# Up products of two half blocks at once in a fused retention and feed-forward kernel

## The chip, the cores and the metric

The kernel runs on one core of one Trainium2 chip. The core has a matrix engine (TensorE, PE in the profile; its weight loads are listed apart as PEld), three engines for elementwise work (VectorE or DVE, ScalarE or ACT, GpSimd or POOL) and SyncE (SP), which here only starts transfers. Each engine takes its instructions in the order of its own queue and waits on semaphores for the others. Matrix products are written to PSUM, 8 banks of 512 float32 in each of 128 partitions; everything else lies in SBUF. The metric is the time of one execution on the device in microseconds (us), taken as the median of the runs.

## The reference

Retention over 4 batches, 8 heads, 768 tokens and head dimension 64 gives a matrix of 3072 tokens by 512. A feed-forward layer follows, 512 to 2048 and back, with g = h - tanh(h) in between. The change lies in the feed-forward layer.

```python
def _attn_ref(q, k, v):
    ...
    for t in range(S):
        state = gamma[None, :, None, None] * state + np.einsum('bhd,bhe->bhde', k[:, :, t], v[:, :, t])
        y[:, :, t] = scale * np.einsum('bhd,bhde->bhe', q[:, :, t], state)

def _moe_ref(x, w_in, w_out):          # x: 3072 x 512, w_in: 512 x 2048, w_out: 2048 x 512
    h = x @ w_in
    g = h - np.tanh(h)
    return (g @ w_out).astype(np.float32)
```

## The kernel before

**Tiling.** The 3072 tokens are 6 blocks of 512, each of two half blocks n of 256 tokens (n = 0 to 11). The 2048 inner columns are 8 pairs m2 of two 128-column groups. A tile (n, m2) is h for 256 tokens and 256 inner columns: one PSUM bank, 128 partitions by 512. For each tile there is an up product (x times w_in), the elementwise part ("shrink", h - tanh(h)) that leaves g in SBUF, and a down product (g times w_out), which is added up in PSUM over the 8 tiles of a half block (a "run") to 256 tokens by 512 output columns. The inputs' retention part and the weights' preparation run early, beside half blocks 0 to 3; the half blocks 4 to 11 that concern us have nothing else beside them after the first steps.

**Seven products for eight.** From half block 4 on (FAST, FAST_UP), both products use a scheme that multiplies 2 x 2 blocks with seven block products and some sums (Winograd's form of Strassen's method). In the up product, numbers 1 to 7 name the products: up_weights (L750) makes sums of weight blocks once per m2, up_tokens (L761) sums of token blocks once per half block, both on POOL. fast_up (L773) issues products 1, 5, 7, 6 to the four quarters of the tile's bank, each as two calls for the two halves of the contraction, 128 columns wide. Then up_take (L782) copies the bank to SBUF on ACT, up_pairs (L785) adds two quarters of the copy pairwise on POOL, products 2, 3, 4 are added onto the bank, and up_add (L790) adds the POOL result on DVE. The down product has the same seven: fast_sums (L615) makes four sums of g's quarters on POOL, fast_products (L661) issues seven products of 256 columns into half-bank accumulators, and sums_of (L674) and fast_end (L705) combine the accumulators at the end of a run: a copy p1 on ACT, seven adds on DVE, two stores on SP's queue. Of the adds, c11 and v come at once, the other five lie in the list `ending` and end_some (L735) takes one of them in each later step. fast_banks (L632) rotates the accumulators of successive runs over six banks: t (two banks in one tile), y (two), o (two single ones).

**The order.** Everything is recorded by hand (manual_schedule): the order in the source is the order in each engine's queue. The main loop (L989) does a step for each tile: products 1, 5, 7, 6 of this tile; the copy; the last factors of the tile before on ACT and DVE; the pair sums on POOL; the first four down products of the tile that is `lag` = 3 steps back; products 2, 3, 4; up_add; tanh and square; the end of the tile before (multiply, copy_predicated, fast_sums); the remaining three down products; one pending add; then the first DVE operations of this tile. After the last tile the remaining three tiles' down products follow. The very last of them goes through finish (L718), which orders its seven products so that each add can follow early, and takes the quarter c22 by way of ACT and POOL.

**The shrink chain.** For a tile, ACT does tanh, square (u), q0, q1 and large, three of them from u; DVE does th = h - tanh (L502), h = (q0 + C0) h (L506), g = (q1 + A C1) h (L515, shrink_last_factor), g = g u (L522) and copy_predicated (L523). q0 and q1 have one buffer each, u, th and large two. Names in the profile are cut of their numbers: h is a tile's bank, fast_head the ACT copy and its pair sums, fast_t, y and fast_o the accumulators, s the sums of g, sum the output rows.

## Time and profile before

| | |
|---|---|
| median of 3 runs | 696.62 us (696.27 to 698.77) |
| the profiled execution | 695.71 us, of which the span is 693.9 us |
| PE busy in the span | 685.8 us (99%), 6540 instructions |
| DVE, ACT, POOL busy | 523.8 us (75%), 432.6 us (62%), 348.1 us (50%) |
| granted TensorE clock | 1.00 |
| up records of 128 columns (L778) | 28 in each step of half blocks 4 to 11 |
| down records of 256 columns (L669) | 14 in each step of half blocks 4 to 11 |
| POOL 128x256 (L788), 128x512 (L208), 128x128 (L620) | 731, 1325, 458 ns |
| ACT 128x512 copy, tanh, square from u | 586, 598, 725 ns |
| DVE 128x512 L502, L506, L515, L522, L523 (from 500 us on) | 680, 689, 688, 736, 751 ns |
| DVE L793 (128x256), L795 (128x128) | 433, 329 ns |

The span runs from the first to the last instruction of the profiled execution; the execution's own time is 1.8 us longer. A busy time counts the instructions of an engine, not its waits. Matmuls are pipelined: the listed duration of one is longer than the spacing of two that follow each other, so the spacing (a group's time divided by its records) is what a product costs in a full queue. The product issued by one call in the code appears as two records. The other engines overlap a little too: an instruction can start about 0.1 us before the listed end of the one before it.

### The profile page before, as it was taken

The page shows a single profiled execution, that of the slowest core. Times are in us where ns is not written, and L with a number is a line of the kernel's source. Part 1 is how long each engine was busy: PE and PEld are TensorE (multiplying, and loading weights), DVE is VectorE, ACT ScalarE, POOL GpSimd, SP SyncE. Part 2 cuts the span into 40 slices and gives each one's busy share as a digit, 9 for nine tenths or more (in the row PEclk, how much of TensorE's full clock was granted, in tenths as well). Part 3 has the DMA queues.
Part 4 walks back from the last instruction along what each step waited for, and adds up shares of the span by engine and source line. Part 5 has one row for each costly group of instructions (what it writes and reads, how often), then busy time and mean ns, then how long its engine had stood idle before and what let it go on. Part 6 is the DMA issues. An engine that isn't in the chain of part 4 may idle for free.

```text
span 693.9 us, 16487 instructions
## 1 busy us (share of the span) xinstructions
PE 685.8 (99%) x6540; PEld 572.4 (82%) x6540; DVE 523.8 (75%) x894; ACT 432.6 (62%) x818; POOL 348.1 (50%) x517
## 2 busy tenths in 40 slices
PE   8999999999999999999999999999999999999997
PEld 5776666667667767789999999999999999999996
DVE  4999999988988965587777676676676776766775
ACT  4787577766867665555665556655556655556553
POOL 1632454454454677878853354453544543544333
PEclk9999999999999999999999999999999999999999
DMA  8992268869888657400000000000000000000001
GB/s 231 242 281 50 79 172 222 214 166 237 222 189 231 147 153 197 123 33 1 1 1 16 17 1 31 1 1 31 1 1 31 1 5 27 2 16 17 1 16 46
DMA packets 119548, 59.95 MB, mean 86 GB/s; under 512 B 101680, under 2 KB 112560, under 8 KB 119472
## 3 DMA queue, kind: packets, MB, share of 16 engines
q1 hardware_dynamic: 116880, 50.21, 27.9%
q10 hardware_dynamic: 2592, 8.69, 3.4%
q8 instruction: 51, 0.84, 0.5%
q14 instruction: 25, 0.20, 0.1%
HBM read 35.83 MB, written 14.68 MB: 73 GB/s over the span
## 4 chain that ended last, share of the span: by engine, by line
PE 94%; DVE 2%; DMA 2%; issue 1%; ACT 0%; POOL 0%; SPq 0%; POOLq 0%; DVEq 0%; ACTq 0%
PE h L778 28%; PE h L464 16%; PE o L531 16%; PE fast_t L669 10%; PE y L669 8%; PE fast_o L669 8%; PE y L398 3%; PE s L343 2%; PE s L349 1%; DMA k<-in_k_dram 1%; PE kqTp L298 1%; DMA v<-in_v_dram 1%; DMA q<-in_q_dram 0%; DVE a L356 0%; DVE g L523 0%
## 5 line engine op out<-in xcount | busy, mean ns | idle before, releaser
L477 ACT ACTIVATE th<-h 128x512 f32<-128x512 f32 x64 | 38.2, 598 | 141.9 <-DVE h L795 141.9
L620 POOL TENSOR_TENSOR s<-g 128x128 f32<-128x128 f32 x64 | 29.3, 458 | 191.6 <-DVE g L523 185.8
L464 PE MATMUL h<-xT,w 128*128 128x256 f32 x512 | 117.8, 382 | 0.2 <-POOL w L217 0.2
L531 PE MATMUL o<-w,g 128*128 128x512 f32 x256 | 116.5, 596 | 0.0
L464 PEld LDWEIGHTS h<-xT,w 128*128 128x128 f32 x512 | 95.9, 190 | 21.7 <-issue 9.1
L531 PEld LDWEIGHTS o<-w,g 128*128 128x128 f32 x256 | 47.5, 190 | 46.2 <-issue 42.8
L778 PEld LDWEIGHTS h<-xT,w 128*128 128x128 f32 x512 | 76.8, 191 | 8.4 <-ACT fast_head L783 1.0
L523 DVE COPY_PREDICATED g<-large,th 128x512 f32<-128x512 int32 x88 | 76.1, 864 | 9.0
L793 DVE TENSOR_TENSOR h<-h,fast_head 128x256 f32<-128x256 f32 x64 | 27.7, 433 | 68.5 <-PE h L778 65.8
L778 PE MATMUL h<-xT,w 128*128 128x128 f32 x512 | 78.3, 275 | 0.2 <-ACT fast_head L783 0.2
L502 DVE TENSOR_TENSOR th<-h,th 128x512 f32<-128x512 f32 x88 | 60.0, 682 | 18.0 <-ACT th L475 16.6
L515 DVE SCALAR_TENSOR_TENSOR g<-q,h 128x512 f32<-128x512 f32 x64 | 44.0, 688 | 36.5 <-ACT q L491 35.2
L778 PE MATMUL h<-x,w 128*128 128x128 f32 x448 | 68.3, 275 | 0.0
L483 ACT ACTIVATE q<-u,tab 128x512 f32<-128x512 f32 x88 | 63.8, 725 | 1.7
L208 POOL TENSOR_TENSOR low<-low,power 128x512 f32<-128x512 f32 x26 | 34.5, 1325 | 59.2 <-DVE power L201 46.2
L491 ACT ACTIVATE q<-u,tab 128x512 f32<-128x512 f32 x88 | 63.6, 723 | 0.0
L506 DVE SCALAR_TENSOR_TENSOR h<-q,h 128x512 f32<-128x512 f32 x88 | 60.7, 690 | 2.6 <-ACT q L483 2.6
L492 ACT ACTIVATE large<-u,tab 128x512 f32<-128x512 f32 x88 | 62.6, 712 | 0.0
L778 PEld LDWEIGHTS h<-x,w 128*128 128x128 f32 x448 | 59.0, 192 | 0.0
L783 ACT COPY fast_head<-h 128x512 f32<-128x512 f32 x64 | 37.5, 586 | 20.0 <-PE h L778 19.9
L522 DVE TENSOR_TENSOR g<-g,u 128x512 f32<-128x512 f32 x64 | 48.6, 759 | 0.0
L788 POOL TENSOR_TENSOR fast_head<-fast_head 128x256 f32<-128x256 f32 x64 | 46.7, 730 | 1.2 <-ACT fast_head L783 1.2
(197 smaller groups left out, 1494.8 us busy)
## 6 DMA issues: line engine op xcount, KB each, us to landing
rows<-apart ACTq DMA_DIRECT2D x16, 512.0 KB, 4.3
k<-in_k_dram SPq DMA_DIRECT2D x24, 256.0 KB, 4.3
q<-in_q_dram SPq DMA_DIRECT2D x24, 256.0 KB, 4.7
v<-in_v_dram SPq DMA_DIRECT2D x24, 256.0 KB, 5.5
raw<-in_moe_w_out_dram SPq DMA_DIRECT2D x12, 512.0 KB, 4.2
out_dram<-sum SPq DMA_DIRECT2D x22, 256.0 KB, 2.0
raw<-in_moe_w_in_dram SPq DMA_DIRECT2D x14, 256.0 KB, 4.1
raw<-in_moe_w_in_dram SPq DMA_DIRECT2D x28, 128.0 KB, 4.1
```

Of the source, the lines that this page charges most:

```text
L464: nc.tensor.matmul(hp, w1[:, c, ts(2 * m2 + i, P)], xT[n // 2][:, c, ts(n % 2, TH)], start=(begins and c == 0), stop=(c == NC - 1), skip_g ...
L483: nc.scalar.activation(q0, shrinking[n, m2][0], AF.Square, bias=bias0)
L491: nc.scalar.activation(q1, u, AF.Square, bias=bias1, scale=math.sqrt(A))
L492: nc.scalar.activation(large, u, AF.Relu, bias=bias_m)
L502: nc.vector.tensor_tensor(th, hp, th, op=ALU.subtract)
L506: nc.vector.scalar_tensor_tensor(hp, in0=shrinking[n, m2][2], scalar=C0, in1=hp, op0=ALU.add, op1=ALU.mult)
L522: nc.vector.tensor_tensor(flat, src, u, op=ALU.mult)
L523: nc.vector.copy_predicated(flat, large.bitcast(I32), th)
L531: nc.tensor.matmul(o_p[n, j], gT[n, m2][:, i, ts(j, P)], w2[:, 2 * m2 + i], start=(first and i == 0), stop=(last and i == 1))
L669: nc.tensor.matmul(accs[n][k], left[k - 1], right, start=first and k in (1, 6, 7, 4), stop=last, skip_group_check=True)
L778: nc.tensor.matmul(hps[n, m2][:, ts(PLACE[k], P)], s_of[m2][k - 1][:, c], x_of[n][k - 1][:, c], start=(k == 1 and c == 0), stop=(c == 1), ...
L788: nc.gpsimd.tensor_tensor(odd_room[1], first[:, :2], first[:, 3:1:-1], op=ALU.add)
```

## The change

The half blocks 8 to 11 (PAIRED = 8) leave the main loop and get a loop of their own over 16 "block steps": block b (4 and 5), m2 from 0 to 7, in which both half blocks of a block are made at once. The 2 x 2 scheme now splits the 512 tokens of the block into two halves of 256, not the 256 tokens of a half block into two of 128. So a product has 256 columns, and the seven products (14 calls) of a block step fill two banks, one for each half block, with the two inner groups side by side in each. The sums of tokens have four operations per block on 128x512, no longer eight on 128x256, and lie in part in the place of the block's own tokens. The copy is two ACT operations, the pair sums are one POOL operation of 128x512, and the adds are three on DVE of 128x256.

Down products are no longer tied to a tile: next_products(k) issues the next k of the queue of waiting tiles. In half blocks 6 and 7 a step issues 4 + 2 of them (before: 4 + 3). In a block step four are issued after products 1, 7, 5, 6, and more after 2, 4, 3: up to 6 in the first eight block steps and up to 10 in the last eight. They stop at the end of a run. What is left follows after the last block step. feed makes the POOL sums for up to three waiting tiles as soon as their g is there. As g tiles wait longer, new_g takes more room for them: the tokens of finished blocks and a buffer of v, and tiles whose products are done.

The sums at the end of a run are all queued at once in the block loop (end_some(len(ending))). fast_banks gives each run accumulators by name: runs 7, 8, 9 and 10 all have t0, y1, t1 and y0, and the last run has the two o banks and two new ones. For the last run, finish takes the last three tiles accumulator by accumulator, and queues each add behind the products of its accumulator; all seven adds are on DVE, c22 and c21 are stored by ACT's queue and c11 and c12 by SP's.

```diff
...
         hp = hps.pop((n, m2))
         q1 = shrinking[n, m2][3]
-        g = gT[n, m2] = gp.tile([P, 2, TH], F32, tag="g", name=f"g_{n}_{m2}")
+        g = gT[n, m2] = new_g(n, m2)
         dst = hp if n < FAST_UP else g.rearrange("p i t -> p (i t)")
         nc.vector.scalar_tensor_tensor(dst, in0=q1, scalar=A * C1, in1=hp, op0=ALU.add,
                                        op1=ALU.mult)
         shrinking[n, m2].append(dst)
+    units = []
+    def more_units():
+        def of(t):
+            for i in range(4):
+                yield t[:, i].rearrange("p (i t) -> p i t", i=2)
+        yield from of(xp.tile([P, NP, BLK * P], F32, tag="xT", name="g_x2"))
+        for i in range(4):
+            yield gp.tile([P, 2, TH], F32, tag="g", name=f"g_{i}")
+        v_ = inp.tile([P, BANK], F32, tag="v", name="g_v", bufs=4)
+        yield v_.rearrange("p (i t) -> p i t", i=2)
+        for i in range(3, NB - 1):
+            yield from of(xp.tile([P, NP, BLK * P], F32, tag="xT", name=f"g_x{i}"))
+    rooms_for_g = more_units()
+    def new_g(n, m2):
+        if n < PAIRED - 1:
+            return gp.tile([P, 2, TH], F32, tag="g", name=f"g_{n}_{m2}")
+        return units.pop(0) if units else next(rooms_for_g)
     def shrink_end(n, m2):
         u, th, _, _, large, src = shrinking.pop((n, m2))
...
     FAST = 4
+    PAIRED = 8
     PAIRS = NM // 2
     t_of = {}
...
-    spare = []
     accs = {}
+    fast_o = []
     def fast_banks(n):
-        if not spare:
+        if not fast_o:
             t = banks("t", "fast_t")
-            whole = y_banks.rearrange("p two r n t -> p r (two n t)")
-            o = [bank("o", "fast_o") for _ in range(2)]
-            spare.append([t[:, 0], t[:, 1], o[0], whole[:, 0], whole[:, 1]])
-            spare.append(o[1])
-        five, sixth = spare
+            y = y_banks.rearrange("p two r n t -> p r (two n t)")
+            fast_o.extend([bank("o", "fast_o") for _ in range(2)])
+            fast_o.append(dict(t0=t[:, 0], t1=t[:, 1], y0=y[:, 0], y1=y[:, 1],
+                               o0=fast_o[0], o1=fast_o[1]))
+        named = fast_o[2]
         if n == 2 * NB - 1:
-            five[1:3] = five[2], five[1]
-        first, second, third = five[:3]
-        spare[0] = five[3:] + [first, second, third]
+            named.update(h0=bank("h", "last_h"), h1=bank("h", "last_h"))
+        names = {
+            4: "t0 t1 o0 o1", 5: "y0 y1 t0 o1", 6: "t1 o1 o0 y0", 2 * NB - 1: "o0 o1 h0 h1",
+        }.get(n, "t0 y1 t1 y0")
+        first, second, third, sixth = (named[x] for x in names.split())
         acc = {1: first, 2: first, 5: second, 7: second, 3: third, 4: third, 6: sixth}
         right = {2: 1, 7: 1, 4: 1, 6: n % 2}
+        if n == 2 * NB - 1:
+            acc[3], right[3] = sixth, 0
         accs[n] = {k: b[:, ts(right.get(k, 0), TH)] for k, b in acc.items()}
-    def fast_order(n, first):
-        if not first:
-            return (1, 2, 4, 6, 7, 5, 3)
-        return (1, 2, 4, 3, 7, 6, 5) if n == 2 * NB - 1 else (1, 2, 7, 5, 4, 6, 3)
+    def fast_order(first):
+        return (1, 2, 7, 5, 4, 6, 3) if first else (1, 2, 4, 6, 7, 5, 3)
     def fast_down(n, m2, first, last, half=None):
-        some = fast_order(n, first)[{None: slice(7), 0: slice(4), 1: slice(4, 7)}[half]]
+        some = fast_order(first)[{None: slice(7), 0: slice(4), 1: slice(4, 7)}[half]]
         if first and 1 in some:
             fast_banks(n)
         fast_products(n, m2, first, last, some)
...
             "c21": lambda: add(c21, 4, w_, True), "c12": lambda: add(c12, 3, x_),
         }
...
                     store(int(x == "c21"))
             ending.append(step)
-    def finish(n, m2, first, last):
-        todo, store, late_c22 = None, None, None
+    def finish(n, some):
+        todo, store = sums_of(n)
         left, right = (ts(c, TH) for c in range(2))
-        for some, then in (((1, 2), ("p1", "c11")), ((6,), ("v",)), ((7, 5), ("w", "x")),
-                           ((4, 3), ("c21", "c12"))):
-            fast_products(n, m2, first, last, some)
-            if todo is None:
-                todo, store, late_c22 = sums_of(n)
+        for ks, then in (((1, 2), ("p1", "c11")), ((6,), ("v",)), ((7,), ("w",)),
+                         ((4,), ("c21",)), ((5,), ("x", "c22")), ((3,), ("c12",))):
+            for m2 in some:
+                fast_products(n, m2, False, m2 == PAIRS - 1, ks)
             for x in then:
                 todo[x]()
                 if x[0] == "c":
-                    store(int(x[1]) - 1, left if x[2] == "1" else right)
-                if x == "x":
-                    late_c22()
-        store(1, right, nc.scalar)
+                    store(int(x[1]) - 1, left if x[2] == "1" else right,
+                          nc.scalar if x in ("c22", "c21") else nc.sync)
     def end_some(n):
         for _ in range(min(n, len(ending))):
...
                                 u[:, None, :].to_broadcast([P, 2, P]), op=ALU.add)
         nc.vector.tensor_tensor(hp[:, 3], u, w, op=ALU.add)
+    def block_tokens(b):
+        x = xT[b]
+        b11, b12, b21, b22 = (x[:, ds(2 * c, 2), ts(i, TH)] for c in range(2) for i in range(2))
+        room = op.tile([P, 2, 2, TH], F32, tag="sum", name=f"x_block_{b}")
+        t2, t3 = (room[:, i] for i in range(2))
+        t4 = odd_room[3].rearrange("p (b c t) -> p b c t", b=2, c=2)[:, b % 2]
+        x_of["block", b] = (b11, b21, b22, t4, b12, t2, t3)
+        return [
+            lambda d=d, x=x, y=y: nc.gpsimd.tensor_tensor(d, x, y, op=ALU.subtract)
+            for d, x, y in ((t3, b22, b12), (b12, b12, b11), (t2, b22, b12), (t4, b21, t2))
+        ]
+    BLOCK_PLACE = {1: (0, 0), 7: (0, 1), 5: (1, 0), 6: (1, 1), 2: (0, 0), 4: (0, 1), 3: (1, 0)}
+    def block_up(b, m2, some):
+        for k in some:
+            i, place = BLOCK_PLACE[k]
+            for c in range(2):
+                nc.tensor.matmul(hps[2 * b + i, m2][:, ts(place, TH)], s_of[m2][k - 1][:, c],
+                                 x_of["block", b][k - 1][:, c], start=(k in (1, 5) and c == 0),
+                                 stop=(c == 1), skip_group_check=True)
+    def block_take(b, m2):
+        for i in range(2):
+            nc.scalar.copy(out=odd_room[2 * i], in_=hps[2 * b + i, m2])
+    def block_pairs():
+        one, other = (odd_room[2 * i].rearrange("p (i t) -> p i t", i=2) for i in range(2))
+        nc.gpsimd.tensor_tensor(one, one, other[:, ::-1], op=ALU.add)
+    def block_add(b, m2, some):
+        u, w = (odd_room[0][:, ts(i, TH)] for i in range(2))
+        for i, place in some:
+            hp = hps[2 * b + i, m2][:, ts(place, TH)]
+            nc.vector.tensor_tensor(hp, w if i and place else hp, u, op=ALU.add)
     waiting = []
     def part(j, n, m2, first, last):
...
         while len(waiting) > lag:
             tile_ = waiting[0] if half == 0 else waiting.pop(0)
             if tile_[0] >= FAST:
-                if tile_ == steps[-1]:
-                    finish(*tile_)
-                    return
                 fast_down(*tile_, half=half)
                 if tile_[3] and half != 0:
                     fast_end(tile_[0])
...
                 return
...
+    def next_products(k):
+        while k > 0 and waiting and not ended:
+            tile_ = waiting[0]
+            if not begun_down:
+                begun_down.extend(fast_order(tile_[2]))
+                if tile_[2]:
+                    fast_banks(tile_[0])
+            some = begun_down[:k]
+            del begun_down[:k]
+            k -= len(some)
+            made[0] += len(some)
+            fast_products(*tile_, some)
+            if not begun_down:
+                waiting.pop(0)
+                if tile_[0] >= PAIRED - 1:
+                    units.append(gT[tile_[:2]])
+                if tile_[3]:
+                    ended.append(tile_[0])
+                feed()
...
+    def feed():
+        for tile_ in waiting[:3]:
+            if tile_[:2] not in fast_g:
+                if tile_[:2] not in shrunk:
+                    break
+                fast_sums(*tile_[:2])
...
             up_pairs()
             for make in with_sums.get(s, []):
                 make()
-            downs(lag, 0)
+            if n < PAIRED - 2:
+                downs(lag, 0)
+            else:
+                next_products(4)
+                end_run()
             fast_up(n, m2, (2, 3, 4))
             up_add(n, m2)
             shrink_begin(n, m2)
             if before:
                 shrink_end(*before)
                 if before[0] >= FAST:
-                    fast_sums(*before)
-            downs(lag, 1)
-            end_some(1)
+                    shrunk.add(before)
+                    if n < PAIRED - 2:
+                        fast_sums(*before)
+                    else:
+                        feed()
+            if n < PAIRED - 2:
+                downs(lag, 1)
+            else:
+                next_products(2)
+                end_run()
+            end_some(1 + 2 * (n == PAIRED - 1))
             shrink_two(n, m2)
             before = n, m2
             if s + 1 not in with_chunk:
...
             shrink_end(n, m2)
             for make in with_sums.get(s, []):
                 make()
...
+    for n in range(PAIRED, 2 * NB):
+        waiting += [(n, m2, m2 == 0, m2 == PAIRS - 1) for m2 in range(PAIRS)]
+    FIRST_BLOCK = PAIRED // 2
+    tokens = []
+    aim = made[0]
+    for j in range((NB - FIRST_BLOCK) * PAIRS):
+        b, m2 = FIRST_BLOCK + j // PAIRS, j % PAIRS
+        one, other = (2 * b, m2), (2 * b + 1, m2)
+        for i, x in enumerate((one, other)):
+            hps[x] = bank("h", "h_%d_%d" % x) if j % 2 else fast_o[i]
+        block_up(b, m2, (1, 7, 5, 6))
+        block_take(b, m2)
+        block_pairs()
+        near = left_in_run() <= 7
+        next_products(left_in_run() if near else 4)
+        rest(*before)
+        end_run()
+        end_some(len(ending))
+        if m2 == PAIRS // 2 and b + 1 < NB:
+            tokens = block_tokens(b + 1)
+        block_up(b, m2, (2, 4, 3))
+        aim += 10 if j < PAIRS else 14
+        if not near:
+            next_products(min(left_in_run(), aim - made[0]))
+        if m2 >= PAIRS // 2 and tokens:
+            tokens.pop(0)()
+        block_add(b, m2, [(0, 1)])
+        begin(*one)
+        activated(*one, 1)
+        activated(*one, 0)
+        block_add(b, m2, [(1, 0), (1, 1)])
+        begin(*other)
+        activated(*other, 1)
+        shrink_two(*one)
+        end_run()
+        end_some(len(ending))
+        shrink_factor(*one)
+        shrink_third(*one)
+        shrink_factors(*one)
+        shrink_last_factor(*one)
+        shrink_end(*one)
+        shrunk.add(one)
+        feed()
+        activated(*other, 0)
+        shrink_two(*other)
+        shrink_factor(*other)
+        shrink_third(*other)
+        before = other
+    rest(*before)
+    next_products(left_in_run())
+    end_run()
+    end_some(len(ending))
+    LAST = 3
+    next_products(7 * (PAIRS - LAST))
+    finish(2 * NB - 1, [x[1] for x in waiting])
```

The helper functions begin, activated and rest record what shrink_begin and the calls after it record in the main loop, for one tile.

## The prediction

> **What bounds the kernel now.** I read the busy time by stretches first, then the chain of waits, then one step of the timeline, then the end. The stretch from 545.48 to 594.66 us holds eight half-block steps of the part that changes. Its columns are the stretch, its length, the busy time of PE, PEld, DVE, ACT and POOL with the count of instructions, the granted clock, the DMA share and GB/s.
>
> ```profile
> 545.48:594.66 49.18, 49.18 (x338) 46.29 (x338) 34.83 (x64) 29.10 (x50) 22.31 (x44) 1.00 0.03 12
> ```
>
> PE is busy for 49.18 of 49.18 us at the full clock. No other engine is over 71%, so only a change in PE's own work, or a new wait on PE, can move this stage. The chain gives that work's price (start, us, engine, tile, line, records):
>
> ```profile
> 190.56 3.45 PE h L464 x16
> ...
> 643.85 1.78 PE h L778 x16
> 645.63 0.86 PE y L669 x4
> 646.50 0.43 PE fast_t L669 x2
> 646.93 0.43 PE fast_o L669 x2
> 647.36 1.34 PE h L778 x12
> 648.70 0.87 PE y L669 x4
> 649.57 0.43 PE fast_t L669 x2
> ```
>
> The trace has two records for each product the code issues. A step is 28 up records of 128 columns (1.78 + 1.34 = 3.12 us, 111.6 ns each) and 14 down records of 256 columns (3.02 us, 216 ns each). From 545.48 to 643.85 us sixteen steps take 98.37 us, 6.148 each. The up records of 256 columns at L464 cost 3.45 / 16 = 215.6 ns.
>
> **Up products.** Two steps now spend 2 x 3.125 = 6.25 us on 56 up records. A block step has 28 records of 256 columns: 28 x 0.2156 = 6.04 us. That is 0.21 us less, over 16 block steps **3.4 us less**. The nearest rows bound it: some L464 groups stand at 3.65 us (0.228 each), which gives 6.39 us and 2.2 us more in all; half of the 128-column rate is excluded, since no 256-column row is below 0.2156. I take 0.2156, because the L669 records right beside the up records have it too.
>
> The Trainium skill, "TensorE: Matmul & The Clock Gate", section "Back-to-back issue gap", has a load-and-multiply pair at about 81 ns for 128 columns against 56 ns for the multiply alone, so 25 ns of weight loading that a wider product would hide. Over 896 records that would be an estimated 22 us. The rows here show only 111.6 - 215.6 / 2 = 3.8 ns, and decide.
>
> **Work of the other engines in a block step**, by rows (ns). DVE: three 128x256 adds (433) for two L793 (433) and two L795 (329), 1.30 for 1.52 us; the five shrink operations twice, 2 x (680 + 689 + 688 + 736 + 751) = 7.09; 8.4 us together. ACT: copies, tanh, squares and relu as before, 2 x 3.93 = 7.9 us. POOL: eight sums of 458, and one 128x512 add, unseen here: between 1.28 (458 to 731 is 273 for 128 columns, twice more on top of 731) and 1.33 (L208); I take 1.33, the row of that size. That is 5.0 us, 6.3 with a token operation. PE has 6.04 + 10 x 0.4315 = 10.36 us in each of the first eight block steps and 6.04 + 14 x 0.4315 = 12.08 in the last eight, so PE still has the most work. The down products that fall back (one in each step of half blocks 6 and 7, four in each of the first eight block steps) are only moved: nothing, as long as their g tiles and sums are there, and falling back makes these earlier, not later.
>
> **Waits inside a block step.** The timeline of an old step shows the delays (start, us, engine, line, operation; in brackets the idle time and its releaser). Its first four up products end at 583.99:
>
> ```profile
> 584.24 0.59 ACT L783 COPY fast_head<-h 128x512 f32<-128x512 f32 x1 [0.36 <-PE h L778]
> 584.73 0.72 ACT L491 ACTIVATE q<-u,tab 128x512 f32<-128x512 f32 x1
> 585.32 0.73 POOL L788 TENSOR_TENSOR fast_head<-fast_head 128x256 f32<-128x256 f32 x1
> 585.48 0.69 DVE L515 SCALAR_TENSOR_TENSOR g<-q,h 128x512 f32<-128x512 f32 x1 [0.87 <-ACT q L491]
> ...
> 587.32 0.43 DVE L793 TENSOR_TENSOR h<-h,fast_head 128x256 f32<-128x256 f32 x1 [1.16 <-PE h L778]
> 587.79 0.30 DVE L795 TENSOR_TENSOR h<-fast_head 128x128 f32<-128x128 f32 x1
> 588.00 0.69 DVE L522 TENSOR_TENSOR g<-g,u 128x512 f32<-128x512 f32 x1
> 588.19 0.60 ACT L477 ACTIVATE th<-h 128x512 f32<-128x512 f32 x1 [2.13 <-DVE h L795]
> 588.79 0.75 DVE L523 COPY_PREDICATED g<-large,th 128x512 f32<-128x512 int32 x1
> ```
>
> PE to ACT takes 0.25 us, PE to DVE 0.27, ACT to DVE 0.03. Let T be the end of (1, 7, 5, 6). The second copy runs from T + 0.25 to T + 0.84. Products (2, 4, 3) add to the banks that it reads and start after four down products, at T + 1.73: 0.9 us of cover. The previous tile's q1 ends at T + 1.46, its last factor starts at 1.49, the multiply at 2.24, the predicated copy at 3.03, and DVE is free at 3.68; its first add waits for product 4 until T + 3.45 + 0.27 = 3.72. Then come the adds (3.72, 4.59, 5.06), the subtraction (5.40), the third operation (6.83, behind tanh and three more activations), last factor, multiply, predicated copy (7.45, 8.20, 8.99), and the other tile's two (9.64, 10.24), until 10.93. The next last factor is due at 10.36 + 1.49 = 11.85, so 0.9 us are spare, 2.6 in the last eight. No wait in a plain step.
>
> **Waits at a change of run.** The diff gives runs 7 to 10 the same four accumulators, where the old ones rotate. The sums of a run (one copy of 0.375, seven adds) are now queued in one go on DVE between the subtraction and the third operation; behind them stand the shrink chain, its q0 on ACT, and behind that the next copies. By the program's order the copy waits for the run's last product and the new run's first product for the last add, as two of the accumulators are one tile. That is 0.25 + 0.375 + 0.03, then adds that start 0.34 apart, or 0.49 where one needs the one before it (0.43 + 0.06): 2.8 us, and 0.08 back to PE: 3.54 us from the run's last product, against 3.45 of up products in between, 0.09 late. The third operation starts at 0.66 + 2.34 + 0.34 = 3.34 us, q0 behind it at 3.34 + 0.69 + 0.10 = 4.13, the first copy 0.62 later, and it is done for PE at 4.75 + 0.59 + 0.05 = 5.39; product 2 is due at 3.54 + 1.73 = 5.27, so 0.12 more. I put 0.2 us on each of three such changes, 0 to 0.5 by the scatter of these rows. From run 6 to 7 the cover is only 1.78 us of 128-column products, and the copy stands behind tanh and square (1.1 us): about 0.45. The four token operations of the first block are 4 x 1.33 on POOL in one step, 2.4 more than the old 4 x 0.73; the pair sums behind them come late and the next ACT copy has 0.9 us of cover: 0 to 0.4, I take 0. Together **1.1 us more**, from 0 to 2.6.
>
> **The end.**
>
> ```profile
> 689.21 0.59 PE L669 MATMUL fast_o<-w,s 128*128 128x256 f32 x2
> ...
> 690.18 0.42 DVE L686 TENSOR_TENSOR sum<-fast_o,fast 128x256 f32<-128x256 f32 x1
> 690.27 0.73 POOL L701 TENSOR_TENSOR sum<-q,fast 128x256 f32<-128x256 f32 x1 [2.62 <-ACT q L700]
> 691.03 0.34 ACTq L689 DMA_DIRECT2D out_dram<-sum  x1
> ```
>
> The last product ends at 689.21 + 0.43 = 689.64, the span at 693.9: 4.26 us, the last 2.9 after POOL's late quarter is ready at 691.00. After the change the last three products fill one accumulator, and only one add is left: 0.27 + 0.43 + 2.9 = 3.6 us, **0.7 us less**. The other quarters' sums fit under the products of the next accumulator (1.29 us against 0.43 to 0.9 of adds). Two stores move to ACT's queue, where nothing is behind them. If the store on SP's queue is slower this is nothing.
>
> **Sum.** The profiled execution took 695.71 us (span 693.9 and 1.8 around it): 695.71 - 3.4 + 1.1 - 0.7 = 692.7. It lies 0.9 below the median of the runs, 696.62, on whose scale I forecast: 696.6 - 3.0 = **693.6 us**, range of this case 693.1 to 695.6.
>
> **Rivals.** *All waits are hidden* (every margin above is a few tenths, and DVE's starts overlap): 696.6 - 3.4 - 0.7 = 692.5. Against it: the change from run 6 to 7 has 1.78 us of cover for more work than that. *The change of run takes over*: if the sums come late on DVE, PE stands at each of four changes for the chain of 3.5 us, since no spare accumulator is left; 4 x 3.5 = 14 us, 696.6 - 4.1 + 14 = 706.5. It decides from 1.9 us a change (4 x 1.9 = 7.6, which eats 4.1 and 3.5 more). For it: DVE is the fullest engine after PE and the sums stand behind its shrink work. Against: last eight steps have 2.6 us spare. *Wide up products bring nothing* (0.223 a record, between both L464 rows): 696.6 + 1.1 - 0.7 = 697.0.
>
> **Chances.** Forecast 0.51, hidden waits 0.37, change of run 0.09, no gain from width 0.03. Three and a half us is 0.5%, about what a measurement of this kernel can tell from no change; faster by more is the second case (0.37), slower by more the third (0.09), the rest 0.54. The range, 691.9 to 697.3, holds the first two with run-to-run scatter (696.27 to 698.77 before) and the fourth.
>
> **What will show it.** Right: 28 up records of a block step in about 6.04 us; PE's idle time after 545 us in four places, before the first products of a run or before (2, 4, 3), 1.1 us in all; 3.6 us from the last product to the end. Wrong: up records above 0.22 us; PE waiting for ACT's copies in plain block steps, which would mean that DVE's chain is longer than 10.4 us; or over 1 us of PE idle at each change of run.

## The result and the profile after

The changed kernel takes 696.65 us (median of 14 runs, 694.72 to 698.59), the kernel before 696.87 us (14 runs, 695.50 to 698.77). The ratio is 0.9995 with a 95% interval of 0.9984 to 1.0007: no change that can be told from none, where 3.0 us less were forecast. Its profiled run has a span of 694.9 us at a granted clock of 1.00. PE is busy a little less than before, and it now has idle time:

```profile
PE 684.3 (98%) x6092; PEld 556.4 (80%) x6092; DVE 534.2 (77%) x879; ACT 427.3 (61%) x817; POOL 358.3 (52%) x492
```

To find where the time went I cut each trace at two points of PE: the start of the first seven-product group of 128 columns (half block 4) and the end of the last product (the last group's start and 0.2157 us for each of its records). All that the change touches lies between them or behind the second. The busy times of that part, first of before, then of after, with columns as in the prediction's first view:

```profile
284.09:689.64 405.55, 405.37 (x2918) 376.75 (x2912) 284.83 (x510) 236.01 (x412) 203.22 (x382) 1.00 0.04 15
```

```profile
285.87:691.52 405.65, 403.63 (x2470) 361.04 (x2464) 295.48 (x496) 231.13 (x412) 215.23 (x358) 1.00 0.04 15
```

This "late part" took 405.55 us and now takes 405.65. Before, PE was busy in all of it but 0.18 us. After, 2.0 us of it are idle by the listed times (more in truth, as the last matmul before a gap is listed longer than its spacing), and DVE is busy 10.7 us longer although it has 14 instructions fewer and, by the forecast's rows, should have 0.2 us less in each block step. POOL is busy 12.0 us longer, where two 128x256 sums (2 x 0.73) became one of 1.27 us. So single instructions of both became longer; a listed time can include a wait, as shown below.

The late part repeats to 0.1 us from run to run of one kernel, and its start does not: over the ten profiles with the same code up to there it begins anywhere from 284.0 to 287.5 us. That scatter, and not the change, makes this one profile after 1.0 us longer than the one before. So I compare late parts and ends:

| term | forecast | measured |
|---|---|---|
| up products 256 columns wide | -3.4 | -3.36 (16 block steps, 6.04 us each) |
| waits of PE | +1.1 | +3.46 (405.65 less 405.55 - 3.36 = 402.19) |
| late part | -2.3 | +0.10 |
| end, from the last product to the end of the span | -0.7 | -0.88 (3.38 for 4.26) |
| sum | -3.0 | -0.78 |

-0.78 us is inside the interval of the ratio, -1.1 to +0.5 us.

The chain of waits shows an undisturbed block step as predicted, with 3.45 + 2.59 = 6.04 us for 28 up records:

```profile
588.80 3.45 PE fast_o L832 x16
592.25 1.29 PE fast_t L692 x6
593.54 0.43 PE y L692 x2
593.98 2.59 PE fast_o L832 x12
596.57 0.86 PE y L692 x4
597.43 1.73 PE fast_t L692 x8
```

The end, in the timeline, has one add and one store behind the last product:

```profile
690.22 1.46 PE L692 MATMUL last_h<-w,s 128*128 128x256 f32 x6
691.71 0.42 DVE L709 TENSOR_TENSOR sum<-last_h,fast 128x256 f32<-128x256 f32 x1 [0.54 <-PE last_h L692]
692.16 0.33 SPq L712 DMA_DIRECT2D out_dram<-sum  x1
```

The waits of PE from 300 us on (releaser, total us, times, longest):

```profile
PE fast_t L692 <- DVE sum L709: 0.8, 2, 0.5
PE h L793 <- ACT fast_head L798: 0.7, 2, 0.5
PE fast_o L832 <- ACT fast_head L838: 0.5, 1, 0.5
```

From the starts of PE's groups (each group's time less its records times 0.2157, or 0.1116 for 128 columns) the 3.46 us lie here:

| place | lost us |
|---|---|
| fifth step of half block 7, behind the first block's four token operations (in the third) | 0.77 |
| change of run 6 to 7, sixth step of half block 7 and after | 0.79 |
| change of run 7 to 8, fifth block step | 0.14 |
| ninth block step, behind the second block's token operations (in the fifth to the eighth) | 0.75 |
| change of run 8 to 9, tenth block step | 0.80 |
| change of run 9 to 10 | 0.13 |
| all else | 0.08 |

Four of the six places are changes of run, as forecast, and two of the four have the size forecast. But behind the token operations 0.77 and 0.75 us are lost, where nothing was booked, and the change from 8 to 9 costs nearly six times its twin from 7 to 8.

Why can be read in the block steps with token operations. In the fifth (timeline, one POOL and one DVE instruction) DVE's third add, which has both inputs in SBUF, takes 1.11 us beside a token operation, for 0.43 us elsewhere:

```profile
530.49 1.27 POOL L822 TENSOR_TENSOR x_block<-xT 128x512 f32<-128x512 f32 x1
...
530.94 1.11 DVE L848 TENSOR_TENSOR fast_o<-fast_head 128x256 f32<-128x256 f32 x1
```

In the eighth it is three pairs of instructions (the token operation is the second row of POOL, L822):

```profile
559.67 1.27 POOL L842 TENSOR_TENSOR fast_head<-fast_head 128x512 f32<-128x512 f32 x1
559.76 1.72 DVE L543 TENSOR_TENSOR g_x<-g_x,u 128x512 f32<-128x512 f32 x1
560.89 1.72 POOL L822 TENSOR_TENSOR x_first<-xT,x_block 128x512 f32<-128x512 f32 x1
561.59 1.63 DVE L544 COPY_PREDICATED g_x<-large,th 128x512 f32<-128x512 int32 x1
```

The multiply (L522 in the kernel before) takes 1.72 us and not 0.69, the predicated copy 1.63 and not 0.75, and the token operation itself 1.72 and not the 1.27 of the fifth step. Over all instructions of the line (duration min/median/max in ns) the multiply is seldom so slow, and its median hides it:

```profile
L543 DVE TENSOR_TENSOR g_x<-g_x,u x24: 678/692/1724, 444.1 to 664.4; 128x512 f32<-128x512 f32 x24
```

How they become longer can be read from the ends. Each row of the eighth step (the fence with four rows) starts while the one above it, on the other engine, still runs. The pair sums (L842) end at 560.94, the multiply 0.54 us after that, the token operation 1.13 us after the multiply, the copy 0.61 us after the token operation. Each of these is 0.14 us or so less than what the instruction takes undisturbed (0.69, 1.27, 0.75). So each row ends as if it had begun its work when the one above it ended: the two engines take turns, and a listed time is wait and work together. From 400 us on 15 of the 47 multiplies of the changed kernel take from 0.91 to 1.75 us, and every one ends 0.54 to 0.56 us after a POOL operation that was under way when it started, whether that took 0.45 or 1.27 us. None of the other 32 started beside a POOL operation under way. In the kernel before it is 5 of 47 (1.21 us each, 0.54 to 0.55 after the POOL operation).

The collisions cost DVE 0.7 us in the fifth block step, 1.1 in the sixth (the add takes 1.53) and 1.9 in the seventh and the eighth, where the forecast had 0.9 us to spare in a step.

PE feels it in the next two steps. The ninth block step, around the gap before products 2, 4, 3:

```profile
567.50 0.72 ACT L483 ACTIVATE q<-u,tab 128x512 f32<-128x512 f32 x1
567.66 0.59 PE L692 MATMUL y<-fast_kqT,s 128*128 128x256 f32 x2
568.13 1.05 ACT L838 COPY fast_head<-fast_o 128x512 f32<-128x512 f32 x2
568.75 1.13 PE L832 MATMUL fast_o<-xT,w 128*128 128x256 f32 x4 [0.49 <-ACT fast_head L838]
```

PE has given out all its down products at 568.1 (the last group starts at 567.66, two records) and waits for the copy, which starts only at 568.13. In ACT's queue q0 of the eighth step's second tile is ahead of it, and that step's activations are late because DVE is: the first of them, a tanh that waits for DVE's adds, starts at 563.58, 0.67 us after the ninth step's first product, and in the run without token operations below (tok5_none) 2.49 us before it. Then the ninth step's pair sums stand on POOL behind eight late sums of g, DVE waits 1.95 us for them, and the sums of run 8, queued behind that on DVE, are late for the first products of run 9 in the tenth step:

```profile
573.37 1.26 POOL L842 TENSOR_TENSOR fast_head<-fast_head 128x512 f32<-128x512 f32 x1
574.67 0.76 DVE L848 TENSOR_TENSOR fast_o<-fast_o,fast_head 128x256 f32<-128x256 f32 x2 [1.95 <-POOL fast_head L842]
576.59 0.39 ACT L715 COPY fast<-fast_t 128x256 f32<-128x256 f32 x1
579.26 0.42 DVE L709 TENSOR_TENSOR sum<-fast_t,fast 128x256 f32<-128x256 f32 x1
579.82 1.10 PE L692 MATMUL fast_t<-w,g_x 128*128 128x256 f32 x4 [0.45 <-DVE sum L709]
```

### The profile page after: what moved, and what is told of

Its sections match the earlier page's. It is cut to its first block, busy times and chain, and to the rows that moved or that the text cites. A ratio compares the mean times of both kernels' runs of the same rounds, so it can differ in the third digit from the quotient of the medians.

```text
span 694.9 us, 15471 instructions
## 1 busy us (share of the span) xinstructions
PE 684.3 (98%) x6092; PEld 556.4 (80%) x6092; DVE 534.2 (77%) x879; ACT 427.3 (61%) x817; POOL 358.3 (52%) x492
## 4 chain that ended last, share of the span: by engine, by line
PE 88%; DMA 3%; POOL 3%; SPq 2%; ACT 2%; DVE 2%; issue 1%; ACTq 0%; DVEq 0%; POOLq 0%
PE h L464 15%; PE o L552 15%; PE h L793 12%; PE fast_t L692 11%; PE y L692 8%; PE fast_o L832 7%; PE h L832 6%; PE fast_o L692 5%; PE y L398 3%; PE last_h L692 1%; PE s L349 1%; PE s L343 1%; SPq L159 1%; DMA rows<-apart 1%; DMA raw<-in_moe_w_in_dram 1%
## 5 line engine op out<-in xcount | busy, mean ns | idle before, releaser
L464 PEld LDWEIGHTS h<-xT,w 128*128 128x128 f32 x512 | 95.9, 190 | 22.4 <-issue 9.1
L477 ACT ACTIVATE th<-h 128x512 f32<-128x512 f32 x32 | 19.1, 597 | 73.1 <-DVE h L810 73.1
L544 DVE COPY_PREDICATED g<-large,th 128x512 f32<-128x512 int32 x62 | 54.6, 880 | 6.2
L842 POOL TENSOR_TENSOR fast_head<-fast_head 128x512 f32<-128x512 f32 x16 | 21.4, 1339 | 63.9 <-ACT fast_head L838 63.9
L217 POOL TENSOR_TENSOR w<-low,head 128x512 f32<-128x512 f32 x28 | 36.6, 1307 | 14.7 <-DVE low L208 7.6
L793 PEld LDWEIGHTS h<-xT,w 128*128 128x128 f32 x256 | 38.0, 191 | 6.2 <-ACT fast_head L798 1.9
L793 PE MATMUL h<-xT,w 128*128 128x128 f32 x256 | 39.6, 277 | 0.7 <-ACT fast_head L798 0.7
L803 POOL TENSOR_TENSOR fast_head<-fast_head 128x256 f32<-128x256 f32 x32 | 23.4, 730 | 27.5 <-ACT fast_head L798 27.5
L282 POOL TENSOR_TENSOR q<-q,tab 128x512 f32<-128x512 f32 x16 | 17.1, 1066 | 38.7 <-DMA q<-in_q_dram 32.8
L282 POOL TENSOR_TENSOR v<-v,tab 128x512 f32<-128x512 f32 x21 | 24.3, 1157 | 21.3 <-DMA v<-in_v_dram 20.2
L444 ACT COPY xT<-y 128x256 f32<-128x256 f32 x48 | 15.5, 378 | 29.9 <-PE y L398 29.9
```

The lines of the kernel that those rows point to most:

```text
L282: engine.tensor_tensor(out_, t, g, op=ALU.mult)
L464: nc.tensor.matmul(hp, w1[:, c, ts(2 * m2 + i, P)], xT[n // 2][:, c, ts(n % 2, TH)], start=(begins and c == 0), stop=(c == NC - 1), skip_g ...
L544: nc.vector.copy_predicated(flat, large.bitcast(I32), th)
L793: nc.tensor.matmul(hps[n, m2][:, ts(PLACE[k], P)], s_of[m2][k - 1][:, c], x_of[n][k - 1][:, c], start=(k == 1 and c == 0), stop=(c == 1), ...
```

## The experiments

The theories at the start: the token operations on POOL, by holding DVE up, cost the time (against it: the sums at the changes of run alone do); shared accumulators or late sums set the waits at the changes; and, from the start at 285.87, that the change makes the early part longer. All numbers below are of the late part unless said otherwise, since one run gives it to about 0.1 us, where whole times of single runs scatter by some 3 us. The whole times of single runs stand in brackets.

**Both kernels once more**, to see what scatters.

> The kernel before, a second profile. The profiled execution of the changed kernel began its first seven-product step at 285.94 us, the one before at 284.16 us, 1.8 us apart, in code that the change does not touch. If that is scatter from execution to execution, this run's start can lie anywhere from 283.5 to 286.5; if the change causes it, it lies at 284.2 +- 0.3. The late part (from that start to the end of the last product) is 405.5 +- 0.2 us by both.

Measured: start 286.96, 0.5 us beyond the range given for scatter and 2.8 us from the first run's start; late part 405.55 (698.59 us).

> The changed kernel, a second profile. Scatter: the start of the first seven-product step differs from 285.94 by some tenths to 2 us. Caused by the change: 285.9 +- 0.3. The late part is 405.75 +- 0.3 us, with the same five stretches of PE idle time: 0.7 us at the token operations of the first block, 0.6 at the change from run 6 to 7, 0.6 and 0.6 in the ninth and tenth block step, 0.1 at the other changes.

Measured: start 284.64, late part 405.66 (695.77 us). The start of before is now the later one, by 2.3 us, and both late parts come out within 0.01 us of the first. The theory of a longer early part falls.

**Without the second block's token operations** (the last 512 rows are then made from the tokens of the block before).

```diff
-            tokens = block_tokens(b + 1)
+            x_of["block", b + 1] = x_of["block", b]
```

> The second block (the last 512 tokens) uses the token sums of the first block, so its four token operations are left out and the last 512 rows of the output are those of the wrong tokens. Theory A (the token operations on POOL hold up DVE, and all that follows is late): the wait of PE for ACT's copy in the ninth block step (0.65 us) is gone and the change from run 8 to 9 falls from 0.8 to 0.2 us, so the late part is 404.4 +- 0.3 us. Theory C (the sums queued in one go at the change of run do it alone): the ninth and tenth block steps stay as they are, 405.7 us.

Measured: 404.15 (695.46 us), 1.50 us less. That is the ninth step's loss and all of the tenth's but what its twin costs (0.75 + 0.80 - 0.14 = 1.41), though the sums at that change of run are all still made. That the sums alone cause the loss falls. The multiplies of the seventh and the eighth step still take 1.20 and 1.04 us here, beside the pair sums, so that some 0.5 and 0.35 of the 1.9 us are not the token operations' doing.

**Memsets in their place**: POOL works at the same places and about as long (1.46 us), but reads nothing.

```diff
-            tokens = block_tokens(b + 1)
+            x_of["block", b + 1] = x_of["block", b]
+            room = op.tile([P, 2, 2, TH], F32, tag="sum", name="x_memset")
+            tokens = [lambda: [nc.gpsimd.memset(room[:, i % 2], 0.0) for i in range(3)]] * 4
```

> As without the second block's token operations (the last 512 rows come from the first block's token sums), but POOL does three memsets of 128x512 at each of their places, into room that nothing reads. If DVE is held up by what POOL reads from SBUF, memsets, which read nothing, do not slow it: late part 404.15 +- 0.2 us and no multiply (L543) over 1.3 us in these steps. If it is POOL's queue that is late, or any POOL work beside DVE: 405 us or more.

Measured: 404.21 (696.45 us). In the timeline, DVE and POOL in the seventh block step:

```profile
548.05 1.27 POOL L842 TENSOR_TENSOR fast_head<-fast_head 128x512 f32<-128x512 f32 x1
548.65 1.22 DVE L543 TENSOR_TENSOR g_v<-g_v,u 128x512 f32<-128x512 f32 x1
549.25 1.46 POOL L1196 MEMSET x_memset<- 128x512 f32 x3
549.97 0.75 DVE L544 COPY_PREDICATED g_v<-large,th 128x512 f32<-128x512 int32 x1
```

The predicated copy lies wholly beside a busy POOL and takes its usual 0.75 us. The multiply, which starts beside the pair sums, and these read, takes 1.22. The same place in the changed kernel:

```profile
548.55 1.27 POOL L842 TENSOR_TENSOR fast_head<-fast_head 128x512 f32<-128x512 f32 x1
548.62 1.75 DVE L543 TENSOR_TENSOR g_v<-g_v,u 128x512 f32<-128x512 f32 x1
549.78 1.72 POOL L822 TENSOR_TENSOR x_block<-xT 128x512 f32<-128x512 f32 x1
550.48 1.63 DVE L544 COPY_PREDICATED g_v<-large,th 128x512 f32<-128x512 int32 x1
```

Here the copy takes 1.63 beside a POOL operation that reads two tiles. The third add (L848) shows the same: beside the memsets of the sixth block step it takes 0.43 us, beside the token operation 1.53. So it is not that POOL is busy, or that its queue is longer: it is that POOL reads.

**The token operations on DVE**, those of the first block one to a step (on POOL this second part alone is tried below).

```diff
...
-            lambda d=d, x=x, y=y: nc.gpsimd.tensor_tensor(d, x, y, op=ALU.subtract)
+            lambda d=d, x=x, y=y: nc.vector.tensor_tensor(d, x, y, op=ALU.subtract)
...
-        for make in block_tokens(PAIRED // 2):
-            make()
+        if not first_ops:
+            first_ops.extend(block_tokens(PAIRED // 2))
+        first_ops.pop(0)()
...
-    with_sums.setdefault(PAIRS * (PAIRED - 1) + 2, []).append(first_block)
+    for i in range(4):
+        with_sums.setdefault(PAIRS * (PAIRED - 1) + 2 + i, []).append(first_block)
```

> All eight token operations on DVE in place of POOL, one a step (those of the first block in four steps of half block 7). Theory A (POOL and DVE hold each other up): DVE gets 0.7 us more work in eight steps, which its spare time (0.9 us and more) takes; PE's idle time at the first block's tokens (0.7 us) and in the ninth and tenth block steps (1.3) is gone, late part 403.8 +- 0.4 us, and no multiply (L543) takes over 1.2 us. Theory B (DVE just has too much to do): 0.7 us more on DVE makes it worse, late part 406 or more. Theory C: 405 to 405.7, only the 0.7 us of the first block are gained.

Measured: 404.18 (693.62 us), 1.47 less, in the range; but not for the reason alone that was given. The part of the first block's tokens is gone, the change from 6 to 7 costs about 0.45 us and not 0.79 (why was not tried), and 0.43 and 0.8 us stay in the ninth and the tenth step. The forecast that no multiply takes over 1.2 us failed:

```profile
556.70 1.26 POOL L842 TENSOR_TENSOR fast_head<-fast_head 128x512 f32<-128x512 f32 x1
556.79 1.72 DVE L543 TENSOR_TENSOR g_x<-g_x,u 128x512 f32<-128x512 f32 x1
558.61 0.74 DVE L544 COPY_PREDICATED g_x<-large,th 128x512 f32<-128x512 int32 x1
559.24 0.68 DVE L822 TENSOR_TENSOR x_first<-xT,x_block 128x512 f32<-128x512 f32 x1
```

It stands beside the pair sums, which read SBUF as well; only the copy is back at 0.74. That collision and 0.7 us of new DVE work in each of four steps are more than DVE has to spare, so the two late steps stay late.

**The same operations earlier**, in the first four block steps.

```diff
-        if m2 == PAIRS // 2 and b + 1 < NB:
+        if m2 == 0 and b + 1 < NB:
             tokens = block_tokens(b + 1)
...
-        if m2 >= PAIRS // 2 and tokens:
+        if tokens:
```

> The second block's four token operations stand in block steps 1 to 4 in place of 5 to 8, still on POOL. Carry: they fall where DVE is not yet late from the change 7 to 8, and DVE has four steps to recover before the next change; the ninth step's 0.75 us go and the change 8 to 9 falls to 0.2, late part 404.4 +- 0.4 us, though the change 7 to 8 may cost some tenths more. If the place does not matter: 405.65 us.

Measured: 404.20 (697.13 us), 1.45 less: as good as leaving them out. There still are collisions (an add of 1.24 us for 0.43 at 500.26), but here DVE is on time and one of them fits into what is spare. Nor do they come in a row: the four token operations keep their 1.27 us, lengthen two adds by 0.8 us each, and no multiply or copy falls beside them.

How late DVE is can be read from one instruction of each block step, the last factor of the tile before (L515): its start less the start of the step's first product, less the 4.89 us of an undisturbed step, worked out from the timelines of five runs:

| block step | 5 | 6 | 7 | 8 | 9 | 10 | 11 |
|---|---|---|---|---|---|---|---|
| change of run in it | 7 to 8 | | | | | 8 to 9 | |
| after | 2.63 | 1.06 | 0.88 | 1.66 | 2.34 | 3.28 | 0.02 |
| tok_dve | 2.63 | 1.42 | 1.18 | 1.64 | 2.03 | 3.27 | 0.02 |
| tok5_none | 2.63 | 0.57 | 0.00 | 0.00 | 0.00 | 2.63 | 0.01 |
| tok5_memset | 2.64 | 0.55 | 0.00 | 0.00 | 0.00 | 2.64 | 0.01 |
| tok_early | 2.63 | 0.57 | 0.00 | 0.00 | 0.00 | 2.63 | 0.02 |

A change of run by itself makes DVE 2.63 us late, which two steps make good, and costs PE 0.14 us. With the token operations behind it DVE isn't on time again by the next change: the 0.88 us of the seventh step grow by 0.7 to 0.8 in each of the next two. In tok_early the steps ahead of the fifth are late by at most 0.08 us.

**The sums of run 6 sooner**, in the steps of half block 7 ahead of the new tile's first DVE operations.

```diff
             up_add(n, m2)
+            if n == PAIRED - 1:
+                next_products(2)
+                end_run()
             shrink_begin(n, m2)
...
-            else:
+            elif n == PAIRED - 2:
                 next_products(2)
                 end_run()
```

> In half block 7 the last two down products of a step and the sums at a run's end are recorded ahead of tanh and square, so that ACT makes the copy p1 before them. PE's wait at the change from run 6 to 7 (0.66 us with what follows) goes; nothing else changes: late part 405.0 +- 0.2 us. If that wait comes from elsewhere: 405.65 us.

Measured: 404.92 (694.80 us), 0.73 less: nearly all of the 0.79 at the change from 6 to 7.

**Two names exchanged** in runs 7 to 10: products 3 and 4, whose accumulator the sums read last, no longer share a tile with products 1 and 2, with which the next run begins.

```diff
-        }.get(n, "t0 y1 t1 y0")
+        }.get(n, "t0 y1 y0 t1")
```

> Runs 7 to 10 get their four accumulators in another order (t0 y1 y0 t1): the tile t then holds products 1, 2 and 6, and products 3 and 4 lie in y. The copy p1 and the first adds no longer wait for the run's last product. By theory C the changes from run 7 to 8, 8 to 9 and 9 to 10 lose their idle time (0.14, 0.8, 0.14 us), late part 404.6 us, and the 0.75 us of the ninth block step stay. If lateness of DVE is carried from the change 7 to 8 through four token operations to the ninth step (theory A with carry), the sums end some 1.2 us earlier there and the 0.75 us go too: 403.8 +- 0.3 us. By theory A without carry the change from 8 to 9 still waits: 405.2 us.

Measured: 405.22 (695.27 us), 0.43 less: the number written beside "theory A without carry", and a miss for the other two, carry included. Both changes of 0.14 us are gone, and the ninth step loses some 0.15 less. The wait for an accumulator in the tenth step is gone too, but PE stands for the copies in the ninth and tenth step:

```profile
567.19 1.13 PE L832 MATMUL fast_o<-xT,w 128*128 128x256 f32 x4 [0.33 <-ACT fast_head L838]
580.14 1.13 PE L832 MATMUL h<-xT,w 128*128 128x256 f32 x4 [0.60 <-ACT fast_head L838]
```

DVE's lateness, as in the table above, is still 2.18 us in the ninth step (2.34 before the exchange); it finds the next thing that waits for DVE. So the number agrees with "theory A without carry" for another reason: the change from 8 to 9 no longer waits for its accumulators, and tok_early shows that lateness is carried.

**The first block's operations one to a step, and all four edits together.** These runs have plain transfers early on, in all four kernels of the group; with them the turning of q and k is left out for 16 of the 24 chunks, so that the output is of other numbers, while the late part has the same instructions:

```diff
-        apart = mid.tile([P, 2, 2, H * D], U16, tag="apart", name=f"apart_{ci}", bufs=1)
+        apart = mid.tile([P, 2, 2 * H * D], U16, tag="apart", name=f"apart_{ci}", bufs=1)
...
-            nc.scalar.copy(out=apart[:, :, which],
-                           in_=words.rearrange("p (n two) -> p two n", two=2))
+            nc.scalar.copy(out=apart[:, which], in_=words)
...
-        nc.sync.dma_start_transpose(
-            out=sides[ci].rearrange("p i n t -> p (i n) t").bitcast(U16),
-            in_=rows.rearrange("p two n -> (p two) n"),
+        nc.sync.dma_start(
+            out=sides[ci].rearrange("p i n t -> p i (n t)").bitcast(U16),
+            in_=rows,
```

> The kernel before with the same plain transfers (the turning of 16 chunks left out): late part 405.55 +- 0.2 us; within 1 us of the changed kernel with plain transfers, and 4 us (0.6%) over the run with four edits by the first theory, 2.5 us or less by the second.

Measured: 405.55; 695.70 us (10 runs, ratio to before 0.9987, 0.9972 to 1.0001).

> The changed kernel with the same plain transfers (the turning of 16 chunks left out), the measure for the run with four edits: late part 405.65 +- 0.2 us as with the transposing transfers, if the early part does not reach into the late one. The run with four edits should be 3.3 us under it by the first theory, under 2 us by the second.

Measured: 405.63; 695.56 us (10 runs, 0.9984, 0.9971 to 0.9997). So the late part is untouched by the early transfers, and the two kernels are again equal.

With the first block's four operations in the third to the sixth step of half block 7 (the last two hunks of the diff on DVE, but on POOL):

> The changed kernel with plain transfers (the turning of 16 chunks left out) and only the first block's four token operations spread, one a step, still on POOL. If the 0.77 us at half block 7 come from four of them in a row in POOL's queue, holding up the pair sums and DVE's multiply and copy, they go: late part 404.9 +- 0.2 us. If one operation is enough to be late: over 405.3 us.

Measured: 404.69 (695.30 us), 0.94 less than after_plain: the 0.77 us at those steps and a little of the waits behind them.

With spreading, tok_early, end_early and names in one:

> Four edits together: the first block's token operations one a step (half block 7, steps 3 to 6), the second block's in block steps 1 to 4, accumulators t0 y1 y0 t1, and the sums of run 6 ahead of tanh. q and k of 16 of the 24 chunks are copied by a plain transfer in place of the transposing one, so the turning of those chunks is left out and the output is of other numbers; the late part has the same instructions. If the waits found are all that the change lost, the late part is its product time, 405.55 - 3.4 = 402.2, to 402.7 us. If the lateness only moves on to the next wait, as with the other accumulators alone, the late part stays over 403.5 us.

Measured: 402.19 us, which is 405.55 - 3.36 to the digit, and in 6 runs 691.92 us (690.88 to 694.52), ratio to the kernel before 0.9937 (0.9912 to 0.9961). Of the part from 400 us on, no wait of PE is listed any more:

```profile
283.51:685.70 402.19, 402.01 (x2470) 361.79 (x2464) 291.88 (x496) 231.39 (x412) 213.00 (x358) 1.00 0.04 15
```

PE is idle for 0.18 us, as before the change. DVE's busy time is still 7.1 us above that of before: collisions remain, and no longer reach PE. Against the medians with the same transfers it is 3.8 us below the kernel before (695.70) and 3.6 below the changed one (695.56).

| kernel | late part | less than 405.65 (plain transfers: 405.63) |
|---|---|---|
| tok_spread_plain | 404.69 | 0.94 |
| end_early | 404.92 | 0.73 |
| tok_early / tok5_none / tok5_memset | 404.20 / 404.15 / 404.21 | 1.45 / 1.50 / 1.44 |
| names | 405.22 | 0.43 |
| best2_plain | 402.19 | 3.44 |

The four edits alone add up to 0.94 + 0.73 + 1.45 + 0.43 = 3.55, so they share only 0.1 us.

## Why the prediction was wrong

**Right.** The price of the up products: 6.04 us a block step, 3.36 in all; the kernel with the four edits shows that this gain is there in full. The rival that width brings nothing falls. The end: 0.88 less for 0.7. The changes of run from 7 to 8 and from 9 to 10: 0.14 and 0.13 us for 0.2. For the change from 6 to 7 the place and the reason (1.78 us of cover are too little) were right, as end_early shows, but not the size: 0.79 (0.73 by experiment) for 0.45. The rival that each change costs 3.5 us falls, as none costs over 0.8, and so does the one that all waits are hidden. The sign "after 545 us in four places" was misplaced: the changes from 6 to 7 and from 7 to 8 lie at 464 and 527 us.

**The step that failed** is the term of the waits, "**1.1 us more**, from 0 to 2.6", which measured 3.46, above its upper bound. (That bound, 2.6, is not the sum of the bounds given for its parts either: 3 x 0.5 + 0.45 + 0.4 = 2.35.) Its parts add up to 1.05, and of the 2.4 us above that 0.77 lie behind the first block's token operations, 0.75 in the ninth step, 0.60 in the change from 8 to 9 and 0.34 in the change from 6 to 7. For the first three, two sentences failed.

*"The four token operations of the first block ... 0 to 0.4, I take 0."* They cost 0.77 us where they are (0.94 by experiment). They were priced as POOL's work alone, 4 x 1.33 us, with a delay for the pair sums behind them. In the trace they don't take 1.33 each:

```profile
450.06 1.80 POOL L822 TENSOR_TENSOR x_block<-xT 128x512 f32<-128x512 f32 x1
450.83 1.64 DVE L544 COPY_PREDICATED g_x<-large,th 128x512 f32<-128x512 int32 x1
451.94 1.62 POOL L822 TENSOR_TENSOR x_first<-xT,x_block 128x512 f32<-128x512 f32 x1
...
455.30 0.73 POOL L803 TENSOR_TENSOR fast_head<-fast_head 128x256 f32<-128x256 f32 x1
...
456.06 0.43 DVE L808 TENSOR_TENSOR h<-h,fast_head 128x256 f32<-128x256 f32 x1 [1.62 <-POOL fast_head L803]
```

Two of the four are stretched, g is late by 0.9 us on DVE, POOL's sums of it stand between the tokens and the pair sums, and DVE's add then waits 1.62 us for the pair sums. How much of the 0.77 us is the collisions and how much POOL's longer queue, which the prediction did see, was not tried: one operation to a step removes both.

*"so 0.9 us are spare, 2.6 in the last eight. No wait in a plain step."* The margin was counted for one step by itself, with the average durations of DVE (736 and 751 ns), and then held against each load by itself: the change of run, the token operations ("5.0 us, 6.3 with a token operation" on POOL, with nothing for DVE), the sums. The 0.9 us themselves were about right (1.1 to 1.2 by the table of lateness: the seventh and eighth steps have 1.9 us of collisions and get 0.7 to 0.8 later). But the second block's operations were given nothing on DVE, where they cost 0.7 to 1.6 us a step (0.7, 1.1, 1.45 and 1.6 against the run without them), and they lie in the four steps in which DVE recovers from the change from 7 to 8. What is left over is carried into the ninth step and into the change from 8 to 9: 0.75 + 0.80 us, where 0.2 were booked. That change costs no more than its twin when the steps ahead of it are quiet. The runs without, with memsets for, and with earlier token operations bring 1.44 to 1.50 us back.

**It was to be seen in the trace before.** The prediction took DVE's prices as averages. The step of half block 6 in which the old token operations (L768) run shows the collision, in the timeline of before:

```profile
403.04 0.73 POOL L768 TENSOR_TENSOR x<-xT 128x256 f32<-128x256 f32 x1
403.34 0.58 DVE L795 TENSOR_TENSOR h<-fast_head 128x128 f32<-128x128 f32 x1
403.73 0.78 POOL L768 TENSOR_TENSOR x<-xT,x 128x256 f32<-128x256 f32 x1
403.84 1.21 DVE L522 TENSOR_TENSOR g<-g,u 128x512 f32<-128x512 f32 x1
```

L795 takes 0.58 us for 0.30, and L522 1.21 for the 0.685 of its median; its longest is 1.22 in this kernel, and L523's longest, in the early part, 1.75 for a median of 0.75. In the old kernel an average hid this, since PE never waited for it.

The Trainium skill, "SBUF — State Buffer", section "Who interferes with whom", says that a DVE instruction with two inputs in SBUF contends with a GpSimd instruction that reads SBUF and not with one that only writes it. The runs agree: beside reads 1.63 us for 0.75, beside memsets 0.75. It says too that the shared pair of ports is an exclusive lock. The rows agree with that as well: both engines' rows become longer (POOL 1.27 to 1.72, DVE 0.75 to 1.63), but each time it is the later one, which ends a fixed time after the other (0.54 to 0.56 us for the multiply), and the first of a row of them keeps its length (1.27 us).

**What stays open.** The four edits together ran only with plain transfers; with the transposing transfers of the changed kernel the combination was not tried, though the late parts of before (405.55 and 405.55) and after (405.65 and 405.63) don't differ between the two kinds. Whether the ninth step would stand still for the collisions of the seventh and eighth alone, with no change of run ahead of them, was not tried; in tok_early, with none ahead, collisions of that size did not arise. Why the change from 6 to 7 cost 0.34 us more than forecast was not tried.

## What to carry to other kernels

Take an engine's durations from the slowest rows of a line as well as from its mean, and look what the other engines do beside the slow ones: elementwise work that is moved or made wider on GpSimd can lengthen VectorE's instructions although VectorE has fewer of them. A margin of a step is spent once: follow how late the fullest engine is from step to step, and put movable work where it is on time, not where it is still making good a disturbance. Where runs scatter more than the change is worth, find two points in the trace that enclose all of it; here 400 us repeated to 0.1 us while whole times scattered by 3.

## What the runs showed of the hardware

VectorE and GpSimd, both reading SBUF, take turns: an instruction with two SBUF inputs that starts while the other engine's operation runs ends a fixed time after that operation's end (multiply 0.54 to 0.56 us, predicated copy 0.61, add of 128x256 0.29, GpSimd 128x512 1.08 to 1.13: in each case 0.14 us or so under its own duration), and its listed time includes the wait. On 128x512 float32: multiply 0.69 to 1.72-1.75 us, predicated copy 0.75 to 1.63, GpSimd subtraction 1.27 to 1.72-1.80; an add of 128x256 goes from 0.43 to as much as 1.53, GpSimd's 128x128 sums from 0.46 to 0.92 and more. Three GpSimd memsets of the same size (1.46 us) leave a predicated copy beside them at 0.75 us. The start of the late part, behind the DMA-heavy beginning of the kernel, lay anywhere from 284.0 to 287.5 us in the same code, and 3 us later or earlier made no difference to the 400 us that followed.
